# Block products between up tiles: reordering the batch transitions of a fused attention and feed-forward kernel

## Chip, cores, metric

The kernel runs on one core of one Trainium2 chip. The metric is the device time of one execution in microseconds (us), median of several runs. Engines are named as in the profile: PE is TensorE's matmul row, PEld its weight loads, DVE is VectorE, ACT is ScalarE, POOL is GpSimd, SP is SyncE. "L559" is line 559 of the kernel file. The line numbers of the changed kernel and of the experiments are shifted by a few: L559, L569, L621, L689 and L745 of the kernel before are L558, L568, L622, L688 and L740 of the changed one.

## The reference

```python
# attention: 8 batches, 16 query heads, 4 key/value heads, 384 tokens, head size 64
attn = softmax(q @ k.T / 8) @ v              # grouped heads
x = attn.transpose(0, 2, 1, 3).reshape(3072, 1024)
# feed-forward: w_in is 1024 x 2048, w_out is 2048 x 1024
h = np.maximum(x @ w_in, 0.0)
out = (h * h) @ w_out
```

## The kernel before

Attention of batch b+1 and feed-forward of batch b are interleaved on TensorE by a generator that hands out feed-forward steps between the heads of attention.

**Two streams.** Almost every matmul uses 64 of the 128 rows of the array. A step has a lower half (rows 0 to 63) and an upper half (64 to 127) that add into the same PSUM bank. The lower half of one step runs beside the upper half of the step before. The Python code keeps a modelled clock for each stream (`lo`, `hi`) and decides from it, when it builds the program, in which order instructions are emitted. Nothing is decided on the chip: the order of each engine's list is fixed when the program is built, and an instruction that needs another engine's result waits on a semaphore.

**Up tiles.** 16 tiles of 128 hidden features a batch. Each tile goes through relu on VectorE, then square on ScalarE:

```python
def done():
    R.add("vector", lambda e: e.tensor_scalar_max(hr[r][:, :], acc[:, 0:S], 0.0), ...)
    def square():
        R.add("scalar", lambda e: e.activation(h2T[b % 2][:, c, :], hr[r][:, :], AF.Square), ...)
        ...                      # then, for some tiles: the sums of the first block
    late.append((clock["hi"] + 750.0, square))
```

**Block products.** From batch 2 on, pairs of 128-token tiles are multiplied by `w_out` with seven instead of eight products (a Strassen scheme; the change calls one such block of two token tiles by two halves of the output a quad). The left sides are parts of `h2T` (the squared activations of a token tile) or sums of them that VectorE makes (`a_sum`, in the trace the tile `a_late`):

```python
left = {1: (x0, 0, i0), 2: (x0, NHC, i0), 4: (x1, NHC, i1), 7: (x1, 0, i1), 3: s4, 5: s1, 6: s2}[n]
right = {1: W11, 2: W21, 3: W22, 4: WT4, 5: W12, 6: WT2, 7: WT3}[n]
```

A batch has three token tiles, so an even batch (2, 4, 6) has one pair and leaves a tile, and an odd batch (3, 5, 7) has two pairs, of which the first begins with the tile left by the even batch.

**Order at a transition.** After the last up tile of a batch the products of its first pair begin, in the order 1, 6, 7, 2, 5, 4, then 3. Product 6 needs the sums, and these need the last up tile's square:

```python
q = block(0)
yield from p1(q)
until(last_up[0])
settle()
for n in range(len(pairs)):
    yield from rest(q)           # 6, 7, 2 (its end queues the next block's sums 1, 2, 3), 5, 4
    ...                          # product 1 of the next block, then product 3 of this one
```

**Output.** Products end in PSUM. VectorE adds, or a ScalarE copy, bring them to one of six `y_sb` buffers, taken in turn, and SyncE's queue stores these. A buffer is written again only after its store has landed.

The softmax here doesn't subtract the row's maximum and nothing guards it: scores larger than these inputs give would overflow.

## Time and profile before

| | |
|---|---|
| time, median of 3 runs | 419.48 us |
| span of the profiled execution | 417.2 us |
| PE busy, granted clock | 407.6 us (98%), 1.0 |
| VectorE / ScalarE busy | 207.1 us (50%) / 216.7 us (52%) |

The page of the profile of the kernel before. The digits of part 2 are busy tenths in 40 equal slices; PEclk is the granted clock of TensorE.

```profile
span 417.2 us, 13267 instructions
## 1 busy us (share of the span) xinstructions
PE 407.6 (98%) x6061; PEld 308.1 (74%) x6061; DVE 207.1 (50%) x455; ACT 216.7 (52%) x284; POOL 48.5 (12%) x62
...
PE   8999999999999999999999998999999999999997
...
PEclk9999999999999999999999999999999999999999
```

PE looks full. It isn't quite: the Trainium skill ("Trainium Kernel Development and Optimization", opening section) says that matmul busy time is a bad metric because matmuls are pipelined, and here PE also counts as busy while only one of the two streams works. So the array's work is counted differently in this document. Every 64-row matmul is given its pitch (0.1625 us for 384 columns, 0.216 for 512, read from the timeline) times one half, and this is spread over the time in which it ran. What is missing to 1 in a slice of half a microsecond is called lost. The matmuls of the whole program add up to 394.2 us of work, so 23.0 us of the span are lost: 11.3 in the first 36 us, 3.5 in the last 7.5, the rest between. The total depends on the pitch taken for the many short matmuls (a recount that gives those of 65 columns 0.027 us finds 387 us of work); the losses at the places below came out the same in the recount to about 0.1 us. (Slices that lose under 7% are left out of the lists below, so lists and spans agree to about 0.3 us only.)

The waits of the weight loads, who waited for whom, in the kernel before. (A gap is longer on PEld than on PE, 1.4 us against 1.0 at 162 us, because on PE it counts from the modelled end of the last matmul.)

```profile
engine line waited for: us in total, times, longest us
PEld sc_ps L500 <- ACT expT L504: 3.2, 7, 0.9
PEld f_ps L689 <- DVE a_late L621: 3.1, 4, 1.4
PEld sc_ps L689 <- DVE a_late L621: 2.4, 2, 1.4
PEld sc_ps L689 <- ACT h2T L569: 2.0, 2, 1.5
...
```

L689 is the block products. In these three lines they waited 7.5 us for sums and squares. The timeline of the kernel before at one such place, in order of time (start, length, engine, line):

```profile
389.71 0.55 DVE L565 TENSOR_SCALAR hr<-f_ps 128x384 f32<-128x384 f32 x1
...
390.21 0.59 PE L689 MATMUL sc_ps<-w_out_sb,h2T 64*128 64x512 f16 x2
390.30 0.52 ACT L569 ACTIVATE h2T<-hr 128x384 bf16<-128x384 f32 x1 [1.14 <-DVE hr L565]
390.85 0.23 DVE L621 TENSOR_TENSOR a_late<-h2T 128x128 bf16<-128x128 bf16 x1 [0.59 <-ACT h2T L569]
391.11 0.22 DVE L621 TENSOR_TENSOR a_late<-a_late,h2T 128x128 bf16<-128x128 bf16 x1
...
391.40 0.39 PE L689 MATMUL sc_ps<-w_late,a_late 64*128 64x512 f16 x1 [0.59 <-DVE a_late L621]
```

Relu, square and two small sums follow each other, and PE has nothing left to do from 390.8 to 391.4. There are six such places, one for each of batches 2 to 7, and together they lose 6.4 us.

### The profile page before, as it was taken

Reading aid. Unit: us, or ns where it says so; the run is one execution under the profiler, and the core shown is the slowest. Engines: PE = TensorE matmul, PEld = TensorE weight load, DVE = VectorE, ACT = ScalarE, POOL = GpSimd, SP = SyncE. Lnnn points to the kernel's source line nnn. Section 1 sums busy time; section 2 is a strip of 40 time slices with the busy share of each in tenths; the row PEclk is TensorE's granted clock in tenths of the full one; section 3 lists DMA queues with packets and bytes.
Section 4 is the critical chain, followed back from the end, with each engine's and each line's share of the span. In section 5 each row is a group of like instructions: output and inputs, shape, how many; then the busy total and the mean of one; then the engine's idle time right before and its main releaser. Section 6 shows DMA issues by size and latency. Waiting matters only on the chain.

```text
span 417.2 us, 13267 instructions
## 1 busy us (share of the span) xinstructions
PE 407.6 (98%) x6061; PEld 308.1 (74%) x6061; DVE 207.1 (50%) x455; ACT 216.7 (52%) x284; POOL 48.5 (12%) x62
## 2 busy tenths in 40 slices
PE   8999999999999999999999998999999999999997
PEld 4666888799777886788776887779766788478553
DVE  2664433297333574446554455446564446345453
ACT  4855864377554666465654466556555563224210
POOL 5841002031003000210003000210000000000000
PEclk9999999999999999999999999999999999999999
DMA  8999999739525940399028960299012311020022
GB/s 231 197 197 202 205 188 182 184 65 171 79 96 63 232 71 11 80 160 149 13 96 83 207 128 11 34 180 169 19 48 97 102 38 22 11 92 2 2 103 101
DMA packets 96104, 45.03 MB, mean 108 GB/s; under 512 B 74416, under 2 KB 90032, under 8 KB 96048
## 3 DMA queue, kind: packets, MB, share of 16 engines
q0 software_dynamic: 34288, 16.65, 32.3%
q1 hardware_dynamic: 58720, 25.28, 29.9%
q10 hardware_dynamic: 3040, 2.26, 1.8%
q8 instruction: 47, 0.77, 0.9%
q14 instruction: 9, 0.07, 0.1%
HBM read 35.65 MB, written 12.58 MB: 116 GB/s over the span
## 4 chain that ended last, share of the span: by engine, by line
PE 91%; DVE 4%; ACT 2%; DMA 1%; issue 1%; ACTq 0%; POOL 0%; DVEq 0%
PE sc_ps L559 18%; PE f_ps L559 17%; PE sc_ps L689 12%; PE po L517 12%; PE f_ps L689 11%; PE sc_ps L500 7%; PE sc_ps L603 5%; PE f_ps L603 4%; PE f_ps L824 2%; DMA w_late<-in_q_dram 1%; DVE a_late L621 1%; PE po L378 1%; ACT expT L504 1%; DVE hr L565 1%; PE sc_ps L361 1%; ACT h2T L569 1%
## 5 line engine op out<-in xcount | busy, mean ns | idle before, releaser
L504 ACT ACTIVATE expT<-sc_ps 128x1152 bf16<-128x1152 f32 x112 | 126.5, 1130 | 102.9 <-PE sc_ps L500 60.5
L559 PE MATMUL sc_ps<-xT,w_in_sb 64*128 64x384 bf16 x976 | 152.0, 322 | 0.0
L559 PE MATMUL f_ps<-xT,w_in_sb 64*128 64x384 bf16 x976 | 148.4, 322 | 0.0
L559 PEld LDWEIGHTS sc_ps<-xT,w_in_sb 64*128 64x128 f16 x976 | 83.7, 94 | 13.0
L559 PEld LDWEIGHTS f_ps<-xT,w_in_sb 64*128 64x128 f16 x976 | 84.2, 94 | 10.9
L569 ACT ACTIVATE h2T<-hr 128x384 bf16<-128x384 f32 x122 | 62.2, 519 | 48.7 <-DVE hr L565 48.0
L517 PEld LDWEIGHTS po<-v_aug,expT 64*128 64x128 bf16 x2016 | 77.4, 94 | 11.5 <-DVE o_sb L527 1.9
L517 PE MATMUL po<-v_aug,expT 64*128 64x65 bf16 x2016 | 81.4, 190 | 0.0
L500 PE MATMUL sc_ps<-qT,kT 64*128 64x384 bf16 x336 | 57.8, 323 | 0.7 <-ACT expT L504 0.5
L565 DVE TENSOR_SCALAR hr<-sc_ps 128x384 f32<-128x384 f32 x61 | 33.9, 556 | 38.4 <-PE sc_ps L559 19.2
L565 DVE TENSOR_SCALAR hr<-f_ps 128x384 f32<-128x384 f32 x61 | 33.9, 556 | 32.9 <-PE f_ps L559 22.1
L689 PE MATMUL sc_ps<-w_out_sb,a_late 64*128 64x512 f16 x192 | 47.1, 376 | 0.0
L603 PE MATMUL sc_ps<-w_out_sb,h2T 64*128 64x512 f16 x192 | 41.6, 376 | 0.0
L603 PE MATMUL f_ps<-w_out_sb,h2T 64*128 64x512 f16 x192 | 40.6, 376 | 0.0
L689 PE MATMUL f_ps<-w_out_sb,h2T 64*128 64x512 f16 x160 | 39.4, 376 | 0.0
L689 PE MATMUL f_ps<-w_late,h2T 64*128 64x512 f16 x160 | 39.0, 376 | 0.0
L525 DVE RECIPROCAL rinv<-po 128x6 f32<-128x6 f32 x56 | 11.0, 196 | 46.6 <-PE sc_ps L603 13.8
L689 PE MATMUL sc_ps<-w_out_sb,h2T 64*128 64x512 f16 x128 | 32.0, 376 | 1.3 <-ACT h2T L569 1.1
L527 DVE TENSOR_TENSOR o_sb<-po,rinv 128x384 bf16<-128x384 f32 x56 | 31.2, 558 | 1.9
L689 PE MATMUL sc_ps<-w_late,h2T 64*128 64x512 f16 x128 | 31.4, 376 | 0.0
L500 PEld LDWEIGHTS sc_ps<-qT,kT 64*128 64x128 bf16 x336 | 25.1, 94 | 6.7 <-ACT expT L504 3.2
L621 DVE TENSOR_TENSOR y_sb<-sc_ps,y_sb 128x512 f32<-128x512 f32 (+1 forms) x21 | 14.4, 685 | 24.7 <-PE sc_ps L689 15.9
(103 smaller groups left out, 423.5 us busy)
## 6 DMA issues: line engine op xcount, KB each, us to landing
out_dram<-y_sb SPq DMA_DIRECT2D x47, 256.0 KB, 2.3
q_next<-in_q_dram POOLq DMA_DIRECT2D x7, 768.0 KB, 12.3
w_in_sb<-in_moe_w_in_dram POOLq DMA_DIRECT2D x8, 512.0 KB, 12.0
w_out_sb<-in_moe_w_out_dram POOLq DMA_DIRECT2D x2, 2048.0 KB, 33.2
k_st<-in_k_dram POOLq DMA_DIRECT2D x7, 192.0 KB, 4.5
v_st<-in_v_dram POOLq DMA_DIRECT2D x7, 192.0 KB, 14.3
xT<-o_sb SPq DMA_TRANSPOSE x56, 2.8
w_late<-in_q_dram ACTq DMA_DIRECT2D x1, 768.0 KB, 8.9
```

The costliest lines, as they stand in the source:

```text
L500: "tensor", lambda pe: pe.matmul(sc_ps[:, i, 0:S], kt[rows, j * 128:(j + 1) * 128], qt[rows, :]),
L504: R.add("scalar", lambda e: e.activation(expT[p % NEX][:, 3 * half:3 * half + 3, :], sc_ps[:, 0:3, 0:S], AF.Exp, scale=0.125), reads=[("sc ...
L517: "tensor", lambda pe: pe.matmul(po_v[:, f % NJ, f // NJ, :], expT[p % NEX][rows, 2 * j + f % 2, f // 2 * 128:f // 2 * 128 + 128], v_aug[b ...
L525: R.add("vector", lambda e: e.reciprocal(rinv_v, po_v[:, :, :, D:D + 1]), reads=["po"], writes=[("rinv", p % 2)])
L527: R.add("vector", lambda e: e.tensor_tensor(o_sb[p % NO][:, :, :, :], po_v[:, :, :, 0:D], rinv_v.to_broadcast([128, NJ, 2, D]), ALU.mult), ...
L559: "tensor", lambda pe: pe.matmul(acc[:, 0:S], w_in_sb[rows, kc, c * 128:(c + 1) * 128], xT[b % NXT][rows, kc, :], start=(h == 0 and kc == ...
L565: R.add("vector", lambda e: e.tensor_scalar_max(hr[r][:, :], acc[:, 0:S], 0.0), reads=[key], writes=[("hr", r)])
L569: R.add("scalar", lambda e: e.activation(h2T[b % 2][:, c, :], hr[r][:, :], AF.Square), reads=[("hr", r)], writes=h2(b, c))
L603: "tensor", lambda pe: pe.matmul(acc, h2T[b % 2][rows, c, i * 128:(i + 1) * 128], w_out_sb[rows, c, jj * 512:(jj + 1) * 512], start=(h == ...
L621: R.add("vector", lambda e: e.tensor_tensor(out_ap, a, b, op), reads=reads, writes=writes)
L689: "tensor", lambda pe: pe.matmul(acc, lhs[rows], right[rows, c], start=(first and h == 0 and c == 0), stop=(h == 1 and c == NHC - 1), skip ...
L824: m = pe.matmul(acc[:, 0:S], w_in_sb[:, kc, c * 128:(c + 1) * 128], xT[b % NXT][:, kc, :], start=(kc == 0), stop=(kc == NKC - 1))
```

## The change

Its intent is to put other work into the six gaps. In an even batch the block products are deferred until two up tiles of the next batch have been issued. In an odd batch the two products of the older token tile, 1 and 2, come first, since they need the previous batch only. They are then evacuated one by one (`alone`), and the sums of the second block, which used to be queued when product 2 ended, are queued when product 7 ends. A pacing table, which says how many feed-forward steps go with one head pair of attention in each batch's phase, is changed as well.

```diff
+    def p1(q, alone=False):
...
+    def p2(q, then=None, alone=False):
+        def c11(acc, key):
+            y = next_y()
+            if alone:
+                add(y, q["u"], acc, key)
+            else:
+                R.add("scalar", lambda e: e.copy(y_sb[y][:, :], acc), reads=[key], writes=[("y", y)])
+            store(y, *q["pair"][0], 0)
...
+    def rest(q, early, follow):
+        def sums_ahead():
+            if follow:
+                sum_part(follow, (1, 2, 3))
+
+        until(lambda: all((n, c) in q["summed"] for n in (1, 2, 3, 4) for c in range(NHC)))
...                                              # product 6
+        def p7(acc, key):
+            add(q["v"], q["u"], acc, key)
+            if early:
+                sums_ahead()
+
+        yield from run(q, 7, bank, True, p7, frees=(bank,))
+        if not early:
+            yield from p2(q, sums_ahead)
...                                              # products 5 and 4, as before
@@ in feed_forward, after the up tiles
+            if pending and n == 1:
+                yield from pending.pop()()
...
+        if not paired:
+            for jj in range(2):
+                yield from row_down(b, jj)
+        elif early:                              # odd batch
+            yield from p1(q, True)
+            yield from p2(q, None, True)
+            yield from down_pairs(q, pairs, True, b < B - 1)
+        else:                                    # even batch
+            pending.append(lambda: down_pairs(q, pairs, False, True))
@@ in all_feed_forward, while the next batch's attention is not ready
                 if carry:
                     yield from carry.pop()()
+                elif pending:
+                    yield from pending.pop()()
@@
-    PACE = {1: (3200.0, 3200.0), 2: (4300.0, 3400.0), 3: (5200.0, 3500.0), **{b: (5800.0, 3800.0) for b in range(4, B + 1)}}
+    PACE = {1: (3200.0, 3200.0), 2: (3700.0, 3100.0), 3: (4200.0, 3300.0), 4: (6100.0, 4300.0), **{b: (5800.0, 3800.0) for b in range(5, B + 1)}}
```

(The same products and sums as before, moved into functions of their own. The wait before product 6 changes too: it tested, in the modelled clock, whether the last up tile was over, and now whether all sums are queued.)

More of the change, by code (lines that the diff above doesn't have):

```diff
@@ L542, in h2, with until, row_up @@
         return [("h2T", b % 2, c, t) for t in (range(NJ) if i is None else (i,))]
-    last_up = [None]
     squared = set()
-    def until(job):
-        while not job["over"]:
+    def until(test):
+        while not test():
             clock["lo"] += 100.0
             catch_up(clock["lo"])
-    def row_up(b, c, r, then=None):
+    def row_up(b, c, r, then=None, final=False):
         i = next_bank()
@@ L575, in done @@
             late.append((clock["hi"] + 750.0, square))
+            if final:
+                upped.add(b)
         lo, hi = ([piece(h, kc) for kc in range(NKC)] for h in range(2))
-        last_up[0] = yield from staged("up", push_steps(lo, hi, done, frees=(i,)))
+        yield from staged("up", push_steps(lo, hi, done, frees=(i,)))
     ys = [0]
@@ L684, in emit @@
                 if not isinstance(left, int):
-                    while (left[0], left[1] + c) not in squared:
-                        clock["lo"] += 100.0
-                        catch_up(clock["lo"])
+                    until(lambda: (left[0], left[1] + c) in squared)
                 return R.add(
@@ L711, in product @@
             yield "down", (f1 - f0) / 512 * 1730
-    def down_pairs(pairs, slots, hold):
-        def add(y_out, y_in, acc, key):
-            tensor_op(y_sb[y_out][:, :], acc, y_sb[y_in][:, :], ALU.add, [key, ("y", y_in)], [("y", y_out)])
-        def p1(q):
-            q["e"] = next_bank()
-            q["u"] = next_y()
-            def done(acc, key):
-                R.add("scalar", lambda e: e.copy(y_sb[q["u"]][:, :], acc), reads=[key], writes=[("y", q["u"])])
-            q["p1"] = yield from product(1, q["pair"], (0, 0, 0), q["e"], True, done)
-        def rest(q):
-            pair, n = q["pair"], q["n"]
-            (x0, i0), (x1, i1) = pair
-            sl = q["slots"] = slots[n]
-            def run(n, bank, first, done, prev=None, frees=()):
-                return product(n, pair, sl, bank, first, done, prev, frees)
-            bank = next_bank()
-            yield from run(6, bank, True, lambda acc, key: add(q["u"], q["u"], acc, key), frees=(bank,))
-            bank = next_bank()
-            q["v"] = next_y()
-            yield from run(7, bank, True, lambda acc, key: add(q["v"], q["u"], acc, key), frees=(bank,))
-            def c11(acc, key):
-                y = next_y()
-                R.add("scalar", lambda e: e.copy(y_sb[y][:, :], acc), reads=[key], writes=[("y", y)])
-                store(y, x0, i0, 0)
-                if n + 1 < len(pairs):
-                    slots[n + 1] = take_sums()
-                    a_sums(pairs[n + 1], slots[n + 1], (1, 2, 3))
-            yield from run(2, q["e"], False, c11, q["p1"], (q["e"],))
-            q["g"] = next_bank()
-            def c22(acc, key):
-                y = next_y()
-                add(y, q["v"], acc, key)
-                store(y, x1, i1, 1)
-                if n + 1 < len(pairs):
-                    a_sums(pairs[n + 1], slots[n + 1], (4,))
-                if q["final"]:
-                    add(q["u"], q["u"], acc, key)
-            q["p5"] = yield from run(5, q["g"], True, c22, frees=(q["g"],) if q["final"] else ())
-            def c21(acc, key):
-                y = q["v"]
-                tensor_op(y_sb[y][:, :], y_sb[y][:, :], acc, ALU.subtract, [key, ("y", y)], [("y", y)])
-                store(y, x1, i1, 0)
-            bank = next_bank()
-            yield from run(4, bank, True, c21, frees=(bank,))
-        def p3(q):
-            x0, i0 = q["pair"][0]
-            def c12(acc, key):
-                add(q["u"], q["u"], acc, key)
-                store(q["u"], x0, i0, 1)
-            if q["final"]:
-                def part(f0, f1):
-                    def fn(acc, key):
-                        u = q["u"]
-                        tensor_op(y_sb[u][:, f0:f1], acc[:, f0:f1], y_sb[u][:, f0:f1], ALU.add, [key, ("y", u)],
-                                  [("y", u, f0)])
-                        store(u, x0, i0, 1, f0, f1, ("y", u, f0))
-                    return f0, f1, fn
-                yield from product(3, q["pair"], q["slots"], None, True, [part(0, 384), part(384, 512)])
-            else:
-                yield from product(3, q["pair"], q["slots"], q["g"], False, c12, q["p5"], (q["g"],))
-        def block(n):
-            return dict(n=n, pair=pairs[n], final=not hold and n == len(pairs) - 1)
-        q = block(0)
-        yield from p1(q)
-        until(last_up[0])
-        settle()
-        for n in range(len(pairs)):
-            yield from rest(q)
-            if n + 1 < len(pairs):
-                follow = block(n + 1)
-                yield from p1(follow)
-                yield from p3(q)
-                q = follow
-        if hold:
-            carry.append(lambda: p3(q))
-        else:
-            yield from p3(q)
@@ new lines, in add, with block, sum_part, run @@
+    def add(y_out, y_in, acc, key):
+        tensor_op(y_sb[y_out][:, :], acc, y_sb[y_in][:, :], ALU.add, [key, ("y", y_in)], [("y", y_out)])
+    def block(pair, final=False):
+        return dict(pair=pair, final=final, slots=take_sums(), summed=set())
+    def sum_part(q, which, c0=0, c1=NHC):
+        a_sums(q["pair"], q["slots"], which, c0, c1)
+        q["summed"].update((n, c) for n in which for c in range(c0, c1))
+    def run(q, n, bank, first, done, prev=None, frees=()):
+        return product(n, q["pair"], q["slots"], bank, first, done, prev, frees)
@@ new lines, in p1, with done @@
+    def p1(q, alone=False):
+        q["e"] = next_bank()
+        q["u"] = next_y()
+        def done(acc, key):
+            R.add("scalar", lambda e: e.copy(y_sb[q["u"]][:, :], acc), reads=[key], writes=[("y", q["u"])])
+        q["p1"] = yield from run(q, 1, q["e"], True, done, frees=(q["e"],) if alone else ())
+    def p2(q, then=None, alone=False):
[6 more added lines that the diff above has]
+            store(y, *q["pair"][0], 0)
+            if then:
+                then()
+        if alone:
+            bank = next_bank()
+            yield from run(q, 2, bank, True, c11, frees=(bank,))
+        else:
+            yield from run(q, 2, q["e"], False, c11, q["p1"], (q["e"],))
@@ new lines, in p3, with c12, part, fn @@
+    def p3(q):
+        x0, i0 = q["pair"][0]
+        def c12(acc, key):
+            add(q["u"], q["u"], acc, key)
+            store(q["u"], x0, i0, 1)
+        if q["final"]:
+            def part(f0, f1):
+                def fn(acc, key):
+                    u = q["u"]
+                    tensor_op(y_sb[u][:, f0:f1], acc[:, f0:f1], y_sb[u][:, f0:f1], ALU.add, [key, ("y", u)],
+                              [("y", u, f0)])
+                    store(u, x0, i0, 1, f0, f1, ("y", u, f0))
+                return f0, f1, fn
+            yield from product(3, q["pair"], q["slots"], None, True, [part(0, 384), part(384, 512)])
+        else:
+            yield from run(q, 3, q["g"], False, c12, q["p5"], (q["g"],))
@@ new lines, in rest, with c22, c21 @@
+    def rest(q, early, follow):
+        x1, i1 = q["pair"][1]
+        def sums_ahead():
+            if follow:
+                sum_part(follow, (1, 2, 3))
+        until(lambda: all((n, c) in q["summed"] for n in (1, 2, 3, 4) for c in range(NHC)))
+        bank = next_bank()
+        yield from run(q, 6, bank, True, lambda acc, key: add(q["u"], q["u"], acc, key), frees=(bank,))
+        bank = next_bank()
+        q["v"] = next_y()
+        def p7(acc, key):
[5 more added lines that the diff above has]
+            yield from p2(q, sums_ahead)
+        q["g"] = next_bank()
+        def c22(acc, key):
+            y = next_y()
+            add(y, q["v"], acc, key)
+            store(y, x1, i1, 1)
+            if follow:
+                sum_part(follow, (4,))
+            if q["final"]:
+                add(q["u"], q["u"], acc, key)
+        q["p5"] = yield from run(q, 5, q["g"], True, c22, frees=(q["g"],) if q["final"] else ())
+        def c21(acc, key):
+            y = q["v"]
+            tensor_op(y_sb[y][:, :], y_sb[y][:, :], acc, ALU.subtract, [key, ("y", y)], [("y", y)])
+            store(y, x1, i1, 0)
+        bank = next_bank()
+        yield from run(q, 4, bank, True, c21, frees=(bank,))
@@ new lines, in down_pairs @@
+    def down_pairs(q, pairs, early, hold):
+        if not early:
+            yield from p1(q)
+        while q:
+            follow = block(pairs[0], not hold and len(pairs) == 1) if pairs else None
+            pairs = pairs[1:]
+            yield from rest(q, early, follow)
+            early = False
+            if follow:
+                yield from p1(follow)
+            if follow or not hold:
+                yield from p3(q)
+            else:
+                carry.append(lambda q=q: p3(q))
+            q = follow
@@ L835, in up_step @@
         return "up", (k1 - k0) * 165
+    pending = []
     def feed_forward(b):
@@ L844, in feed_forward @@
         order = list(range(first, NFC))
-        pairs, slots, then = [], {}, {}
+        pairs, then, q = [], {}, None
         if paired:
@@ L850, in feed_forward @@
                 pairs.append((rows.pop(0), rows.pop(0)))
-            slots[0] = take_sums()
+            q = block(pairs.pop(0))
             for c0, c1 in ((0, 4), (4, NHC - 1), (NHC - 1, NHC)):
-                then[2 * c1 - 1] = lambda c0=c0, c1=c1: a_sums(pairs[0], slots[0], (1, 2, 3, 4), c0, c1)
+                then[2 * c1 - 1] = lambda c0=c0, c1=c1: sum_part(q, (1, 2, 3, 4), c0, c1)
+        early = q and q["pair"][0][0] < b
         for n, c in enumerate(order):
             if by_rows[0]:
-                yield from row_up(b, c, tiles[0] % NHR, then.get(n))
+                yield from row_up(b, c, tiles[0] % NHR, then.get(n), n == len(order) - 1)
             else:
@@ L868, in feed_forward @@
                 w_sums(*w_todo.pop(0))
-        last = last_up[0]
-        for kind in down_pairs(pairs, slots, b < B - 1) if paired else (k for jj in range(2) for k in row_down(b, jj)):
-            yield kind
-            if last["over"]:
-                upped.add(b)
+        if not paired:
[5 more added lines that the diff above has]
+            yield from down_pairs(q, pairs, True, b < B - 1)
+        else:
+            pending.append(lambda: down_pairs(q, pairs, False, True))
     def all_feed_forward():
```

## The prediction

> **What bounds the kernel now.** TensorE. The page gives PE 407.6 of 417.2 us busy (98%) at granted clock 1.0. The Trainium skill ("Trainium Kernel Development and Optimization", opening section) warns that matmul busy time misleads because matmuls are pipelined. It does here: every large matmul uses 64 rows, two run side by side, and PE counts as busy when only one half works. So I counted work by pitch: in the timeline a 64-row matmul of 512 columns starts every 0.216 us on each half (the skill's "TensorE: Matmul & The Clock Gate", Part 1, gives 215.7 ns at full clock; the trace agrees), one of 384 columns every 0.1625 us. All matmul records at their pitch, halved for the two halves, sum to 394 us. So about 23 us are unused array: about 11.5 in the first 36 us (loads), 3.5 in the last 7, about 7.7 between.
>
> **Where.** Of those 7.7 us, 6.3 lie at six places, one for each of batches 2 to 7, where the last up tile is followed by block products: 1.3 us at 162, 0.4 at 204, 1.4 at 258, 1.05 at 301, 1.2 at 354-357, 1.1 at 390. The waits view names the releasers: DVE a_late sums four times, ACT h2T squares twice. The timeline at 389-391 shows why: relu 0.55 us, square 0.52, sums of 0.23 each, with handovers about 2.1 us after the last up matmul; the only cover is the first product (1.73 us on each half) and what its successor can do before its eighth piece.
>
> **Removed, added, moved.** Matmul work is unchanged (394.3 us in both orders). In odd batches (3, 5, 7) products 1 and 2 of the older token tile need only the previous batch, so they run while the last relu, square and sums finish: 1.73 us more cover against stalls of 0.4 to 1.1. In even batches (2, 4, 6) two up tiles of the next batch (1.3 us each on each half) come between: 2.6 us more cover against 1.2 to 1.4. In the instruction order the two up tiles do come first in all three cases, and that batch's attention ends early enough for its transposes (2.8 us to landing). Three ScalarE copies (0.58 us) become VectorE adds (0.69 us): VectorE is 50% busy, so free. New pacing moves attention of batches 2 and 3 forward (phases shorter by about 3 and 6 us of work). Scores following their predecessor by under 1.3 us of work cost 0.2 to 0.3 us each now (78, 111, 130 us); the new order has as many, plus or minus one. Start and tail are unchanged.
>
> **Sum.** -6.3 us of stalls, +0.4 for new small waits: -5.9, so **413.6 us**; 8 in 10: **412.0 to 416.5**. Chances: faster by over 2% 0.04 (all gaps between start and tail are 7.7 us, 1.8%), within 2% 0.94, slower by over 2% 0.02.
>
> **Right if:** span near 411.3 us; PE waits for a_late and h2T under 1 us in all (now 3.8); the six gaps absent; matmul count and clock as now; tail unchanged but 6 us earlier.
>
> **Wrong if:** an up tile of the next batch waits for its transposed attention (xT loads, start of batches 3, 5, 7); tighter attention makes scores wait for exp; the early sums of the second block (1024 columns, VectorE) delay the freeing of accumulators; or k and q of the following batch arrive late. Each shows as a PE wait.

## The result

The changed kernel took 416.91 us (median of 6 runs, 416.68 to 417.20) and the kernel before 419.78 us in the same rounds (6 runs). The ratio is 0.9931, with a 95% interval of 0.9918 to 0.9944. About 2.9 us were gained where 5.9 were predicted, and the time lies just outside the predicted range (412.0 to 416.5). The two profiled executions differ by 2.0 us only (spans of 417.2 and 415.2): the profiled run of the kernel before took 419.18 us, 0.6 less than its median here. Where the other 0.9 us lie, the traces do not show.

The page of the changed kernel:

```profile
span 415.2 us, 13254 instructions
## 1 busy us (share of the span) xinstructions
PE 407.2 (98%) x6061; PEld 307.3 (74%) x6061; DVE 206.6 (50%) x458; ACT 214.1 (52%) x281; POOL 48.7 (12%) x62
...
PE   8999999999999999999999899999999999999997
...
PEclk9999999999999999999999999999999999999999
```

The count of matmuls, the clock and the work (394.2 us) are what they were. The weak slice of PE has moved: the 8 that stood in the 25th slice (250 to 261 us, the transition of batch 4) is now in the 23rd, at 228 to 239 us. The waits of the weight loads in the changed kernel:

```profile
engine line waited for: us in total, times, longest us
PEld sc_ps L500 <- ACT expT L504: 4.8, 8, 1.5
PEld po L517 <- DVE o_sb L527: 2.2, 3, 1.0
...
PEld sc_ps L688 <- DVE y_sb L622: 0.8, 1, 0.8
```

No block product waits for sums (a_late) or squares (h2T) of the transitions any more: those 7.5 us are gone from the list. The same place as above, batch 7, in the timeline of the changed kernel:

```profile
388.34 0.52 ACT L568 ACTIVATE h2T<-hr 128x384 bf16<-128x384 f32 x1 [1.14 <-DVE hr L564]
...
388.89 0.22 DVE L622 TENSOR_TENSOR a_late<-h2T 128x128 bf16<-128x128 bf16 x1 [0.59 <-ACT h2T L568]
...
389.15 0.22 DVE L622 TENSOR_TENSOR a_late<-a_late,h2T 128x128 bf16<-128x128 bf16 x1
...
390.44 0.38 PE L688 MATMUL f_ps<-w_late,a_late 64*128 64x512 f16 x1
```

The last of these is the eighth piece of product 6, which needs the small sums: they now end about 1 us before it, and it waits for nothing. In place of the 7.5 us stand longer waits of the scores for exp (L500; the longest was 0.9 us and is 1.5), of the attention products for o_sb (L517; three waits of which the longest is 1.0 us, where there were seven of at most 0.3), and a wait for a y_sb add. The places, with the lost array time of both profiled executions:

| place | before, us lost | changed, us lost |
|---|---|---|
| six transitions, batches 2 to 7 | 1.31 + 0.37 + 1.36 + 1.05 + 1.22 + 1.08 = 6.4 | 0.9 |
| 213.5 us and 313 us: attention product waits for o_sb | 0 | 0.73 + 0.53 |
| 397.5 us: block product waits for an add to y_sb | 0 | 0.55 |
| 229.5 us: scores wait for exp | 0 | 1.47 |
| scores close behind their predecessor | 0.9 | 1.3 |

So the transitions gave 5.5 us, and about 3.7 us were given back elsewhere (0.73 + 0.53 + 0.55 + 1.47 + 0.4). The predicted terms were 6.3 and 0.4.

Three of the new places in the timeline of the changed kernel. First at 213:

```profile
211.57 0.68 DVE L622 TENSOR_TENSOR a_late<-h2T 128x1024 bf16<-128x1024 bf16 x1
212.29 0.69 DVE L622 TENSOR_TENSOR a_late<-a_late,h2T 128x1024 bf16<-128x1024 bf16 x1
...
212.90 0.69 DVE L622 TENSOR_TENSOR h2T<-h2T 128x1024 bf16<-128x1024 bf16 x1
...
213.50 0.19 DVE L525 RECIPROCAL rinv<-po 128x6 f32<-128x6 f32 x1
213.72 0.56 DVE L527 TENSOR_TENSOR o_sb<-po,rinv 128x384 bf16<-128x384 f32 x1
...
214.33 0.20 PE L517 MATMUL po<-v_aug,expT 64*128 64x65 bf16 x1 [0.53 <-DVE o_sb L527]
```

The reciprocal and the product that free the attention accumulator `po` stand in VectorE's queue behind the three 1024-column sums of the second block; the last matmul into `po` had ended at 211.4. At 397 the same three sums stand ahead of an add that frees a PSUM bank, though the product that it adds had ended at 396.3:

```profile
396.68 0.68 DVE L622 TENSOR_TENSOR h2T<-h2T 128x1024 bf16<-128x1024 bf16 x1
397.28 0.68 DVE L622 TENSOR_TENSOR y_sb<-sc_ps,y_sb 128x512 f32<-128x512 f32 x1
...
398.02 0.39 PE L688 MATMUL sc_ps<-w_out_sb,a_late 64*128 64x512 f16 x1 [0.30 <-DVE y_sb L622]
```

Then at 229:

```profile
229.17 0.58 ACT L740 COPY y_sb<-f_ps 128x512 f32<-128x512 f32 x1 [2.64 <-PE po L517]
...
229.65 1.14 ACT L504 ACTIVATE expT<-sc_ps 128x1152 bf16<-128x1152 f32 x1
...
230.84 0.34 PE L500 MATMUL sc_ps<-qT,kT 64*128 64x384 bf16 x2 [1.28 <-ACT expT L504]
```

ScalarE idled 2.64 us before the copy of product 2 of the second block, and exp ran only after it. The profile names PE as what ended that wait. But product 2's last matmul had ended at 226.9, and the copy also waits for the store of the y buffer that it will write. The trace's completion records have that store issued at 221.40 and landed at 229.09, 7.7 us later, where the median of all stores is 2.3. The name in the bracket is the last event that the profile found; that the store was the one that mattered is what two runs below test. The scores that this exp reads had been computed by 227.2.

### The profile page after: what moved, and what is told of

It reads as the page before. It is cut to its first block, busy times and chain, and to the rows that moved or that the text cites. A ratio compares the mean times of both kernels' runs of the same rounds, so it can differ in the third digit from the quotient of the medians.

```text
span 415.2 us, 13254 instructions
## 1 busy us (share of the span) xinstructions
PE 407.2 (98%) x6061; PEld 307.3 (74%) x6061; DVE 206.6 (50%) x458; ACT 214.1 (52%) x281; POOL 48.7 (12%) x62
## 4 chain that ended last, share of the span: by engine, by line
PE 91%; DVE 4%; ACT 2%; DMA 1%; issue 1%; ACTq 0%; POOL 0%; DVEq 0%
PE sc_ps L558 18%; PE f_ps L558 17%; PE sc_ps L688 12%; PE po L517 12%; PE f_ps L688 11%; PE sc_ps L500 7%; PE sc_ps L604 5%; PE f_ps L604 4%; PE f_ps L843 2%; DMA w_late<-in_q_dram 1%; ACT expT L504 1%; PE po L378 1%; DVE y_sb L622 1%; PE sc_ps L361 1%; PE sc_ps L300 1%
## 5 line engine op out<-in xcount | busy, mean ns | idle before, releaser
L558 PE MATMUL f_ps<-xT,w_in_sb 64*128 64x384 bf16 x976 | 150.2, 322 | 0.0
L558 PE MATMUL sc_ps<-xT,w_in_sb 64*128 64x384 bf16 x976 | 149.2, 322 | 0.0
L558 PEld LDWEIGHTS sc_ps<-xT,w_in_sb 64*128 64x128 f16 x976 | 81.8, 94 | 16.0
L558 PEld LDWEIGHTS f_ps<-xT,w_in_sb 64*128 64x128 f16 x976 | 82.6, 94 | 13.3
L517 PEld LDWEIGHTS po<-v_aug,expT 64*128 64x128 bf16 x2016 | 77.4, 94 | 12.2 <-DVE o_sb L527 2.2
L517 PE MATMUL po<-v_aug,expT 64*128 64x65 bf16 x2016 | 81.4, 190 | 0.8 <-DVE o_sb L527 0.8
L500 PE MATMUL sc_ps<-qT,kT 64*128 64x384 bf16 x336 | 56.9, 323 | 2.0 <-ACT expT L504 1.8
L688 PE MATMUL sc_ps<-w_late,h2T 64*128 64x512 f16 x176 | 43.5, 376 | 0.0
L604 PE MATMUL sc_ps<-w_out_sb,h2T 64*128 64x512 f16 x192 | 41.6, 376 | 0.0
L604 PE MATMUL f_ps<-w_out_sb,h2T 64*128 64x512 f16 x192 | 40.6, 376 | 0.0
L688 PE MATMUL f_ps<-w_out_sb,a_late 64*128 64x512 f16 x160 | 39.5, 376 | 0.0
L688 PE MATMUL f_ps<-w_out_sb,h2T 64*128 64x512 f16 x144 | 35.4, 376 | 0.0
L688 PE MATMUL sc_ps<-w_out_sb,h2T 64*128 64x512 f16 x144 | 35.4, 376 | 0.0
L500 PEld LDWEIGHTS sc_ps<-qT,kT 64*128 64x128 bf16 x336 | 25.0, 94 | 8.9 <-ACT expT L504 4.8
L688 PE MATMUL f_ps<-w_late,h2T 64*128 64x512 f16 x112 | 27.2, 376 | 0.0
L688 PE MATMUL sc_ps<-w_out_sb,a_late 64*128 64x512 f16 x112 | 26.9, 376 | 0.3 <-DVE y_sb L622 0.3
```

Source lines behind the costliest of these rows:

```text
L500: "tensor", lambda pe: pe.matmul(sc_ps[:, i, 0:S], kt[rows, j * 128:(j + 1) * 128], qt[rows, :]),
L517: "tensor", lambda pe: pe.matmul(po_v[:, f % NJ, f // NJ, :], expT[p % NEX][rows, 2 * j + f % 2, f // 2 * 128:f // 2 * 128 + 128], v_aug[b ...
L558: "tensor", lambda pe: pe.matmul(acc[:, 0:S], w_in_sb[rows, kc, c * 128:(c + 1) * 128], xT[b % NXT][rows, kc, :], start=(h == 0 and kc == ...
L604: "tensor", lambda pe: pe.matmul(acc, h2T[b % 2][rows, c, i * 128:(i + 1) * 128], w_out_sb[rows, c, jj * 512:(jj + 1) * 512], start=(h == ...
L688: "tensor", lambda pe: pe.matmul(acc, lhs[rows], right[rows, c], start=(first and h == 0 and c == 0), stop=(h == 1 and c == NHC - 1), skip ...
```

## The experiments

The theory, called A below: the transitions were closed as predicted, and the gain was given back by two in-order queues. On VectorE the wide sums stand in front of short instructions for which PE waits. On ScalarE a copy stands in front of exp and waits for a late store. The rival, B: the new pacing packs attention too tightly and takes the gain back, and what stands in front is chance. Array times "lost" are always from the profiled execution. Every run was correct. The runs were made in four groups, each on one chip, with the kernel before in the same rounds (medians 419.6 to 419.9 us).

### Spread the sums in halves

```diff
         def p7(acc, key):
             add(q["v"], q["u"], acc, key)
-            if early:
-                sums_ahead()
+            if early and follow:
+                sum_part(follow, (1, 2, 3), 0, NHC // 2)
 ...
-            if follow:
+            if follow and early:                        # at the end of product 5
+                sum_part(follow, (1, 2, 3), NHC // 2, NHC)
+            elif follow:
                 sum_part(follow, (4,))
 ...                                                     # and sum 4 at the end of product 4
```

> Theory A (given back on VectorE and ScalarE queues: the three 1024-column sums of the second block, queued right behind product 7's add, hold up a reciprocal at 213 and 313 us and an add at 397 us for which PE waits): the three stalls, 1.8 us together in the changed kernel, fall to under 0.6 us; the stall at 229-231 us (1.5 us) stays; time 415.3 to 416.1, about 1.2 us under the changed kernel's 416.9. Rival B (tighter attention pacing is the cause, the sums stand in the way by chance): other VectorE or ScalarE work takes their place, under 0.4 us gained, 416.5 to 417.2.

Measured: 418.24 us (416.66 to 420.93), ratio 0.9972 (0.9939 to 1.0004). The stalls at 213 and 397 us went to zero, but the one at 313 grew from 0.53 to 0.78, so 0.8 us stayed where under 0.6 was expected, and the 1.4 us at 229 stayed too. The time does not show the gain, and it is not one number: three runs had a granted clock of 1.0 and took 416.7 to 417.1 us, three had 0.995 or 0.996 and took 419.4 to 420.9. None of these last three was profiled. What follows: the sums are what held up 213 and 397; the time is inconclusive. The profile says more. It reached the first scores (L500) at 37.06 us, the changed kernel at 35.85, and from there to its end took 378.2 us against 379.4: 1.2 us less, as expected, but hidden by a later start. In the 16 profiles this start lies between 35.8 and 38.0 us, so one span alone proves little. The clock comes back with the quarters below.

### Another output buffer

The copy takes the buffer that was stored longest ago. `second` marks the second block of an odd batch. The edit changes no order on any engine.

```diff
         def c11(acc, key):
             y = next_y()
+            if q.get("second"):
+                y = next_y()
```

> Same order on PE; only the output buffer of the second block's product 2 differs (the one stored longest ago). Theory A says that the copy at 229 us waits for the store of its buffer, which landed 7.7 us after its issue, and that exp and then the scores wait behind that copy: the 1.5 us stall at 229-231 us goes, all others stay, time 415.3 to 415.7 (1.3 to 1.5 us under 416.9). Rival B (pacing puts the scores too close after each other there): the stall stays at 1.0 us or more, time 416.5 to 417.1.

Measured: 415.88 us (415.50 to 418.20), ratio 0.9921 (0.9901 to 0.9941). The stall at 229 us is gone and those at 213, 313 and 397 stayed to a hundredth or two (0.73, 0.54, 0.55). ScalarE's timeline at that place, which lies later here:

```profile
229.06 0.59 ACT L742 COPY y_sb<-f_ps 128x512 f32<-128x512 f32 x1 [0.39 <-PE f_ps L688]
229.54 1.14 ACT L504 ACTIVATE expT<-sc_ps 128x1152 bf16<-128x1152 f32 x1
```

The copy waits for product 2 alone. The median is 0.2 above the expected range, and the ratio's interval overlaps that of the changed kernel (0.9918 to 0.9944), so it is the trace that decides here. The profiled execution (417.61 us) is a slow example: it started later (first scores at 37.2 us), and it shows a wait of 0.7 us at 97 us that no other profile has: one VectorE sum of weights took 1.95 us there instead of 0.68. Its cause is open. The slowest run (418.2) had a clock of 0.996.

### Both

> Both edits. Theory A: the gains add, 2.4 to 2.9 us under the changed kernel: 413.9 to 414.6, close to the predicted 413.6. Rival B: no better than the better of the two alone, above 415.2.

Measured: 415.24 us (4 runs, 414.83 to 415.82), ratio 0.9897 (0.9882 to 0.9911). The profiled execution spans 413.0 us, with 0.25 us lost at 229 and 0.78 at 312. The median misses the expected range by 0.6 us and B's bound (above 415.2) is just met by the number; the interval also overlaps that of the other buffer alone. But of the stalls that A named only the one at 312 is left at its size (at 213 and 397 there is none), so B's reason is not met.

### The changed order with the old pacing

```diff
-    PACE = {1: (3200.0, 3200.0), 2: (3700.0, 3100.0), 3: (4200.0, 3300.0), 4: (6100.0, 4300.0), ...}
+    PACE = {1: (3200.0, 3200.0), 2: (4300.0, 3400.0), 3: (5200.0, 3500.0), ...}    # as before
```

> The changed order with the pacing table of before. Rival B (the new pacing gives the gain back): about 413.6. Theory A: the stall near 397 us, where no attention runs any more, stays at 0.4 to 0.6 us; scores that follow their predecessor by only 0.62 us of work, once, cost 0.7 us; whether a store lands late before a copy depends on when the loads fall; in sum 416 to 418.5, not under 415.5.

Measured: 419.36 us (419.10 to 419.54), ratio 0.9990. B is wrong: it expected about 413.6, and without the new pacing nearly the whole gain is gone. A's range was too low as well, for a reason that it did not contain. In this program's instruction order the block products of batches 2 and 4 follow their own up tiles at once, because the next batch's attention is not ready when they are due; only batch 6 is deferred. The transitions at 161 to 164 us and 257 to 264 us lose 1.3 and 2.8 us again. Near 260 us a half of product 1 runs alone, an artefact that the next section explains, so part of the 2.8 us is this run's own. The stall near 397 (here at 400) is there with 0.55, and the close scores cost 0.8 at 272, about as expected. The pacing is a part of the change that the deferral needs.

### Halves of the change, first try

The even batches run `down_pairs` at once instead of appending it to `pending` (even_off), or the odd ones run it without the two early products (odd_off).

```diff
-            pending.append(lambda: down_pairs(q, pairs, False, True))
+            yield from down_pairs(q, pairs, False, True)                 # even_off
```

```diff
-            yield from p1(q, True)
-            yield from p2(q, None, True)
-            yield from down_pairs(q, pairs, True, b < B - 1)
+            yield from down_pairs(q, pairs, False, b < B - 1)            # odd_off
```

> Only the odd batches are changed. The gaps of the even batches (1.3, 1.4, 1.2 us) come back: 2.5 to 4 us above the changed kernel unless the late store misses its copy now; 418 to 420.5, so no gain over before is left.

> Only the even batches are changed; the odd ones begin with product 1 and run 6, 7, 2 as before. Theory A: the three gaps of odd batches come back (2.5 us less the 0.7 us that is left of them now), but the three stalls behind the wide sums (1.8 us) go or shrink, so this half of the change bought next to nothing: within 1 us of the changed kernel, 416.3 to 417.8. Against it: if the odd half works as predicted, without it the time is 2.5 us worse, 419 to 420.

> The changed kernel itself once more, so that the others can be held against it on one chip: 416.4 to 417.4; the stalls at 213, 229, 313 and 397 us are there again (0.7, 1.5, 0.5, 0.55 us), since they are a matter of order and not of chance.

Measured, in one group: the changed kernel again 416.73 us (ratio 0.9922), odd_off 419.50 (0.9990), even_off 422.86 (1.0069). Both halves came out worse than expected, odd_off even in the range of the view that speaks against A (419 to 420), since neither undoes its part cleanly. The changed `rest` waits, in the modelled clock, until all sums are queued, and so it emits the whole upper half of product 1 before product 6. In the timeline of even_off at 358 to 361 us the two run one after the other on half an array each. The transitions of the even batches lose about 6 us there, against 3.9 in the kernel before. These two runs therefore measure an artefact of their own as well and decide nothing; the clean ones follow below. The changed kernel's stalls at 213, 229, 313 and 397 were there again, with 0.73, 0.86, 0.54 and 0.55 us (after_again). So the three behind the sums repeat to a hundredth, and the one behind the late store varies.

### The sums in quarters, and the other buffer

Two quarters of the sums at the end of product 7 and two at the end of product 5, the second of each pair 0.8 us later in the modelled clock, together with the buffer of the run before:

```diff
+        def quarters(f, *starts):
+            for k, c in enumerate(starts):
+                late.append((clock["hi"] + 800.0 * k, lambda c=c: sum_part(f, (1, 2, 3), c, c + NHC // 4)))
+            settle(clock["hi"])
```

> The sums of the second block in four quarters, two after product 7 and two after product 5, and the other output buffer. Theory A: no VectorE instruction waits more than about 0.7 us behind sums, so what is left at 313 us in the run with halves (0.8 us) falls under 0.4 us, and 213, 229, 397 stay clear: span 412.5, time 413.9 to 414.6, about 2.5 us under the changed kernel. Rival: quarters cost VectorE more fixed time and the stalls only move: not under 415.

Measured, in the same group: 414.46 us (4 runs, 414.44 to 414.67), ratio 0.9870 (0.9857 to 0.9883), 2.3 us under the changed kernel. At 213 and 397 us next to nothing is left (none, and 0.06), at 229 0.05, at 311 0.39. This is the best version. The waits of PE in this run:

```profile
...
PE sc_ps L500 <- ACT expT L504: 0.5, 1, 0.5
PE po L378 <- DVE o_sb L391: 0.3, 1, 0.3
PE po L517 <- DVE o_sb L527: 0.2, 1, 0.2
...
```

(The three lines left out are waits of the start.)

Its interval lies below those of the changed kernel and of the other buffer alone, so here the gain is clear in the time as well. The prediction's sum, 413.6, is what the kernel nearly reaches once the two queues are out of the way.

### Halves of the change, undone cleanly

As the first try, but for the half that is undone the wait in `rest` is that of the kernel before:

```diff
+        if <the block of the undone half>:
+            until(lambda: last_job[0]["over"])      # the last up tile's upper half is queued
+            settle()
         until(lambda: all((n, c) in q["summed"] ...
```

The third run is the kernel before with only the new pacing table, and the fourth has the quarters without the other buffer.

> The even half undone cleanly (the first run of this kind let product 1's second half run alone before product 6 and cost 2 us of its own): even batches as before, odd ones as changed, new pacing. Theory A: the even gaps are back (about 3.9 us), the odd ones stay closed (2.5 to 0.7), the stalls behind the wide sums stay (1.8), a late store may or may not stall: 419.8 to 421.3, so the odd half alone, with the new pacing, gains nothing over before or loses up to 1.5 us. If the odd half were worth its 2.5 us on its own: 417 to 418.

> The odd half undone cleanly: odd batches as before, even ones deferred, new pacing. Odd gaps back (2.5 us), even ones closed; no stall above 0.3 us at 213 and 397 us, since the sums stand behind product 2 again, whose own evacuation is ScalarE's. Theory A: within 1.2 us of the changed kernel, 416.7 to 418.2. If the odd half is worth its 2.5 us: 419 to 420.

> The kernel before with the new pacing table and nothing else. Theory A: the pacing is only there to have the next batch's attention ready; the six gaps stay (6.3 us, give or take 1), 0.4 us of new waits of scores: 419.3 to 420.8, no gain. If pacing itself brings the gain: 417.5 or less.

> Quarters of the sums alone, output buffers as in the changed kernel. Theory A: the stalls at 213, 313 and 397 us fall to 0.5 us together, the one at 229 us stays at 0.9 to 1.5 us: 1.0 to 1.6 us under the changed kernel, 415.1 to 415.9, and above the run with both edits (414.5) by 0.7 to 1.4 us.

Measured, in one group:

| | median, us | ratio to before (95%) | step by the ratio |
|---|---|---|---|
| pacing alone | 421.90 | 1.0055 (1.0032 to 1.0079) | +0.0055, about +2.3 us |
| pacing and odd half | 420.88 | 1.0029 (1.0016 to 1.0042) | -0.0026, -1.1 us |
| pacing and even half | 417.84 | 0.9954 (0.9940 to 0.9968) | -0.0101, -4.2 us |
| all (from the first, another group) | | 0.9931 (0.9918 to 0.9944) | -0.0124, -5.2 us, from pacing alone |

The two clean halves fell into the ranges that A gave. Their steps add up to the whole within 0.1 us: 2.3 - 1.1 - 4.2 = -3.0, measured -2.9. The odd half is worth about 1.1 us net, though it closes gaps of over 2 us; the wide sums that it moved cost 1.8. (The intervals of the first two rows overlap. From the other side, all less pacing and even half, the odd half comes to 0.0023 or 1.0 us, across two groups.) Pacing alone was expected at 419.3 to 420.8 and is slower than that. With it and the old order the gap of batch 3 is 1.4 us instead of 0.4, and the scores at 232 us wait 0.7 us for exp. So the wait for a late store comes with the pacing, not with the new order: in this run, too, the store of that buffer, issued at 224.0, landed at 230.9, and in the run of pacing and even half, where 1.0 us is lost at this place, the profile itself names the store. (In the kernel before stores among the loads took up to 9.1 us as well, but PE lost nothing there.)

The run with quarters alone was expected at 415.1 to 415.9 and took 417.98 (416.18 to 419.19), three of its six runs at a clock of 0.995. This time the profiled one was among them. ScalarE's longest wait in its profile from 224 to 232 us, and the windows around it (length; busy us and instructions of each engine; granted clock; DMA share; GB/s):

```profile
ACT y_sb L740 <- DMA out_dram<-y_sb: 3.9, 1, 3.9
```

```profile
226.00:228.50 2.50, 2.50 (x52) 1.90 (x50) 0.75 (x2) 0.00 (x0) 0.00 (x0) 1.00 1.34 218
228.50:231.50 3.00, 0.55 (x18) 0.34 (x14) 0.69 (x1) 1.62 (x2) 0.00 (x0) 1.00 1.38 142
231.50:232.10 0.60, 0.60 (x8) 0.39 (x10) 0.00 (x0) 0.12 (x1) 0.00 (x0) 1.00 1.33 165
232.10:235.40 3.30, 3.30 (x38) 2.48 (x34) 0.69 (x1) 1.01 (x1) 0.83 (x1) 0.52 1.29 149
```

Here the profile names the store itself. It landed 8.9 us after its issue, PE stood still for 2.45 us, and 0.8 us after it began again the granted clock fell to one half for 3.4 us (0.50 from 232.25 to 235.67; the window shown is a little wider). In those the 512-column matmuls started every 0.43 us instead of 0.216. The place lost 4.4 us in all. The Trainium skill describes the mechanism ("TensorE: Matmul & The Clock Gate", Part 1: the clock is halved after about 3.4 us of idleness and in windows of that length). The length and the half agree with this trace; the idle time that set it off was shorter here. This wait was thus paid for twice. In this execution it ate up what the fixed sums gave: PE came earlier and the store landed later after its issue than in the changed kernel. Of the three runs at full clock (416.18, 417.01, 417.28) there is no profile, so why they gain so little stays open.

### Move the loads

What was still open is why the store lands late. In the same microseconds the k, q and v loads of the next batch are in flight (192, 768 and 192 KB, issued at 217 to 219), and behind the store SyncE's queue issues a transpose.

```diff
-            row_attend(n - 1, load_next if c == 1 and 2 <= b < B - 1 else None)
+            row_attend(n - 1, load_next if c == (3 if b == 5 else 1) and 2 <= b < B - 1 else None)
...
-            if c == (4 if b > 1 else 6):
+            if c == ({5: 5}.get(b, 4) if b > 1 else 6):
```

> The changed kernel, but the k, q and v loads of batch 6 are issued about 10 us later (at 227 us instead of 217) and its transposes one head pair later; nothing else. If those loads are what makes the store at 221 us land 7 to 8 us after its issue, it lands in under 3 us here, the copy at 229 us waits for nothing, and the stall of 0.9 to 1.5 us there goes: 415.3 to 416.2, unless the later transposes make a new wait before 255 us. If the store is late for another reason (the transposes on the same queue), it lands late again and the stall stays.

> The changed kernel for comparison on the same chip: 416.4 to 417.4, with the stalls at 213, 229, 313 and 397 us.

Measured, in one group: late_load 416.08 us (415.94 to 417.12; ratio 0.9916), the changed kernel 416.86 (416.66 to 418.56; ratio 0.9928). In the trace of late_load the loads are issued at 225.5 to 227.4, the store of 221.93 lands after 2.2 us, and the stores of 228.1 and 230.7, which now fall among the loads, land after 7.6 and 7.2 us. The lateness went with the loads. The edit moved the transposes of k and q too, so by itself it does not part the two. The landing times of all 16 profiles do: of 642 stores after 45 us with no load open while they were under way none took over 5.1 us, though a transpose of k or q ran beside 127 of them; the 31 that were issued 1.8 to 6 us after a load of q took 6.3 to 9.8 us, every one. ScalarE's timeline in this run:

```profile
227.45 0.58 ACT L740 COPY y_sb<-f_ps 128x512 f32<-128x512 f32 x1 [0.39 <-PE f_ps L688]
227.93 1.14 ACT L504 ACTIVATE expT<-sc_ps 128x1152 bf16<-128x1152 f32 x1
```

The copy follows product 2 at once, and the stall at 229 us is gone. The other three stalls are unchanged (0.70, 0.54, 0.55). The time is in the expected range, but the intervals of the two ratios overlap (0.9903 to 0.9929 and 0.9916 to 0.9940): again the trace decides. The slowest run of the changed kernel in this group (418.56, clock 0.996) is the profiled one; its clock was 0.83 on average from 10 to 20 us, during the loads at the start. So a lowered clock can come from the start, too.

## Why the prediction was wrong

**Right.** What bounds the kernel, and the cause of the six gaps: the transitions lost 6.4 us before (6.3 in the prediction's count) and 0.9 after, and no wait for sums or squares at them is left. The work is the same (394.2 us), and so are matmul count and clock. The two up tiles came first in all three even batches. The closely spaced scores cost 0.4 us more, which is the whole +0.4 of the prediction.

**The step that failed** is the term "+0.4 for new small waits" of the sum "-6.3 us of stalls, +0.4 for new small waits: -5.9". In its place stand 3.7 us in the profiled execution: the 0.4 of the scores, 1.8 behind the wide sums, and 1.5 behind the late store (0.9 and 0.8 in the two other profiles of the changed kernel). Taking the last two away (the quarters and the other buffer) brought 414.46 us.

- *The wide sums.* The prediction named them under "wrong if" and put no number on them, although the trace before had it. After the change three sums of 0.69 us follow product 7's own add of 0.69, so VectorE is taken for about 2.6 us from the end of product 7, while product 5 ends 1.73 us later and needs an add at once (at 397: product 7 ends at 394.5, product 5 at 396.3, the sums at 397.4). The prediction wrote "VectorE is 50% busy, so free" of three other adds; that reads an average where the order in the queue decides.
- *The late store.* Not foreseen. The prediction looked for k and q arriving late; they came in time, and it was the stores beside them that were late. It did not mention the six output buffers, nor how long a store takes to land among loads.
- *The pacing.* In the prediction it moves attention forward and has no term of its own in the sum. Alone it costs 2.3 us; with it the even half is worth 4.2 and the odd half 1.1. That it is needed for the deferral is shown by the run with the old pacing.
- *The tail.* It is as before (3.5 us lost, then 3.6), but it comes 2 us earlier, not 6.

**Left open.** Why single runs have a clock of 0.995 or 0.996 where no profile was taken (an estimate: one stretch of 3.4 us at half clock, as in the two profiles that have one, lowers the mean over the span by 0.4%); the wait at 97 us that one run showed; and the 0.9 us that remain at the transitions.

## What to carry to other kernels

When work is moved into the gaps of the bounding engine, look at every queue whose order moves with it and ask, for each short instruction that frees something, what now stands in front of it and for how long. An engine that is half idle on average can still be late, and a long instruction there should be cut into pieces no longer than the slack of what waits behind it. A buffer that waits for its store counts with the landing time under load (here 6.3 to 9.8 us), not with the time of a quiet queue (2.3). A stall can also be charged twice if it is long enough to lower the clock, as the one of 2.45 us was here.

## What the Trainium skill lacked or had wrong

- "TensorE: Matmul & The Clock Gate" (the table of "Why this matters for your kernels") advises no PE-idle gaps over about 3 us between matmuls, as one idle window lowers the clock. In the run with quarters alone a gap of 2.45 us was followed by 3.4 us at half clock. In the trace's clock records the low stretch begins at 232.25, so the stretch of the same length before it (from 228.83) holds the whole gap. The waits of up to 1.5 us in the profile of the changed kernel lowered nothing.
- "DMA: Bandwidth & Descriptors" ("Issuing engines are not separate DMA queues") says that DMAs of all queues interleave on the same 16 engines; it gives no size for what that does to a single store. Here a 256 KB store lands in 2.3 us in the median and in 6.3 to 9.8 us when it is issued 1.8 to 6 us after the 768 KB load of q (7.7 in the changed kernel, 9.8 in the run with halves and the other buffer).
- "TensorE: Matmul & The Clock Gate" (its table at the head) calls ScalarE's and VectorE's queues strict FIFO, which agrees with the runs. It has no number for the price: an exp whose scores were there at 227.2 us started at 229.65, behind one copy, and a reciprocal of 0.19 us stood behind 1.9 us of sums.
